# Where the first head's tiles lie: region order, a split weight load and an earlier product in a one-core decode kernel

## The chip, the cores and the metric

The kernel runs on one core of one Trainium2 chip. The metric is device time in microseconds (us). The core has a matrix engine (TensorE, "PE" in the profile, with its weight loads shown apart as "PEld"), VectorE ("DVE"), ScalarE ("ACT"), GpSimd ("POOL") and SyncE ("SP"), which here does nothing but issue loads. All engines run at once and wait for each other through semaphores. Loads from the chip's memory are carried by 16 DMA engines.

## The reference

One token of a decoder passes through an attention block and a gated MLP, and a scalar gate mixes the two:

```
g   = sigmoid((x * gate_w).sum())                       # x: 1 x 1024
q   = x @ wq                                            # 32 heads of 128
p   = softmax(q . k / sqrt(128))                        # 4 KV heads, 65536 cached rows
a   = (p @ v) @ wo
z   = gelu(x @ w_in)                                    # 1 x 3584, halves z1 and z2
u   = z1 * (w_sp * layernorm(z2) + b_sp)
b   = u @ w_out                                         # 1792 x 1024
out = g * a + (1 - g) * b
```

The caches `k_cache` and `v_cache` are bfloat16 of shape (1, 4, 65536, 128), 64 MiB each; 8 query heads share one of the 4 KV heads. The weights are 8 MiB (wq), 8 MiB (wo), 7 MiB (w_in) and 3.5 MiB (w_out). Every byte is read once, and there is one token to use it for.

## The kernel before

Almost everything that is loaded goes into one large buffer `kv` of 4 regions, 4 MiB each (32 KB in each of 128 partitions). The helper `load` issues a load on SyncE's queue into the place `at`, counted in regions; `load_kv` does it for one K tile (16,384 cache rows, one region) or a pair of V tiles (two regions). SyncE issues the loads in the order of the program. A load waits there until the earlier load into its region has landed and all its readers are done; loads behind it wait with it. The order of instructions on each engine is that of the program text (the last lines pin it).

The stages, in order:

- **w_in** in two halves to regions 2 and 3 (line 187), **wq** in one load to regions 0 and 1 (line 189). `x_rows` multiplies x with the first four of the eight row groups and then with the other four, so that two half views `wq_t` exist of the one load (line 190). From the products come `uT`, the vector for w_out, and `qs`, the queries, from which `build_w` makes the weights of the score matmuls.
- **Four KV heads**, g = 0 to 3, of NT = 4 K tiles each. `k_tile` (line 377) transposes a tile in four pieces on VectorE (line 383, the last reader of the region) and multiplies them on TensorE into `s_ps` (line 389); ScalarE copies the scores to SBUF (line 400).
- After a head's fourth tile, `stats` (line 403) finds the maximum over the scores. It needs TensorE twice: a transpose into `mt_ps` (line 408) and a matmul into `nb_ps` (line 415). Then come four exponentials on ScalarE (line 422) and four transposes on VectorE (line 425) that give `pt`.
- From the second head on, the V tiles of the head before are loaded in pairs into regions 2 and 3 and multiplied with `pt` in `v_tile` (line 435), beside the K tiles of the current head, which alternate between regions 0 and 1. `head_out` finishes a head.
- For the first head there are no V tiles yet, so its four K tiles use all four regions, in the order 2, 3, 0, 1 (line 488). After its statistics comes the load of **w_out** into region 2 and its product, 56 matmuls of `project` (line 477).
- **wo** in six loads, the last ones small, its product, and the output.

Of the kernel before, what the change touches and what calls it, by code (L numbers as in the profile page):

```python
# [17 lines left out]
NKV = 4  # L18
# [10 lines left out]
def kernel(  # L29
# [17 lines left out]
    _, _, D = A_x.shape  # L47
    _, G, S, DH = A_k_cache.shape
    HD = A_wq.shape[1]
# [4 lines left out]
    KC = D // P  # L54
    FC = FH // P
    OC = HD // P
    QD = P // H
    NT = S // (P * CT)
# [21 lines left out]
    def same_weights(ins):  # L80
        held.add(ins.ins.name)
# [77 lines left out]
    def load(src, shape, at):  # L159
        n = 1  # L160
        for s in shape:
            n *= s
        v = kv[:, int(at * CT * P):int(at * CT * P) + n]
        if len(shape) == 2:
            v = v.rearrange("p (a b) -> p a b", b=shape[1])
        ins = nc.sync.dma_start(out=v, in_=src)  # L166
        if not first_load:
            first_load.append(ins.ins.name)
        return v

    def load_kv(src, g, j, at, n=1):
        k0, m = j * CT * P, n * CT
        v = load(src[0, g, k0:k0 + m * P, :].rearrange("(p c) d -> p (c d)", c=m),
                 (m * DH,), at)
        return [v[:, i * CT * DH:(i + 1) * CT * DH] for i in range(n)]
# [9 lines left out]
    KH = KC // 2  # L185
    win_view = B_w_in.rearrange("(p c) n -> p c n", c=KC)
    win_t = [load(win_view[:, i * KH:(i + 1) * KH, :], (KH, F), 2 + i) for i in range(2)]
    wq_view = A_wq.rearrange("(p c) n -> p c n", c=KC)
    wq_a = load(wq_view, (KC, HD), 0)
    wq_t = [wq_a[:, i * KH:(i + 1) * KH, :] for i in range(2)]  # L190


    row = const.tile([P, P], FP32, name="row")
# [136 lines left out]
    uT = const.tile([P, FC], BF16, name="uT")  # L330
# [9 lines left out]
    for k in range(NHB):  # L340
# [3 lines left out]
                                                                   j=B, e=2),  # L344
# [20 lines left out]
    def build_w(g):  # L365
        for v in range(VC):
            nc.vector.tensor_tensor(
                out=wt[g % 2][:, v, :, :, v, :],
                in0=qs[:, g].unsqueeze(2).to_broadcast([P, BP, NB, REP]),
                in1=own_n[:].unsqueeze(1).unsqueeze(3).to_broadcast([P, BP, NB, REP]),  # L370
                op=ALU.mult)
# [5 lines left out]
    def k_tile(g, j, kn):  # L377
        kb = kn.bitcast(I32)
        n = CC * DH // 2
        s_ps = pss.tile([P, 2 * HN], FP32, name="s_ps", tag="s")  # L380
        for v in range(VC):
            kt = ktp.tile([P, CC * DH], BF16, name="kt")
            nc.vector.transpose(out=kt[:].bitcast(I32), in_=kb[:, v * n:(v + 1) * n])  # L383
            while late:
                nc.vector.reduce_max(**late.pop())  # L385
            kx = kt[:].rearrange("p (c h k e) -> p h e c k", h=2, k=B, e=2)
            for b in range(BP):
                for k in range(2):
                    ins = nc.tensor.matmul(  # L389
                        s_ps[:, k * HN:(k + 1) * HN],  # L390
                        lhsT=wt[g % 2][:, v, b].rearrange("p a v h -> p (a v h)"),
                        rhs=kx[:, b // 2, b % 2, k * CC // 2:(k + 1) * CC // 2, :],
                        start=(v == 0 and b == 0), stop=(v == VC - 1 and b == BP - 1),
                        skip_group_check=True)
                    if k > 0:
                        same_weights(ins)
        if j == 0:
            mxs[g] = wk.tile([P, NT], FP32, name="mx")
        sct[g, j] = scp.tile([P, CC * B], BF16, name="sc")
        nc.scalar.copy(out=sct[g, j][:], in_=s_ps[:])  # L400
        late.append(dict(out=mxs[g][:, j:j + 1], in_=sct[g, j][:], axis=AX.X))

    def stats(g):
        nc.vector.reduce_max(**late.pop())  # L404
        m1 = wk.tile([P, 1], FP32, name="m1")
        nc.vector.reduce_max(out=m1[:], in_=mxs[g][:], axis=AX.X)  # L406
        mt_ps = psm.tile([1, P], FP32, name="mt_ps", tag="m")
        nc.tensor.transpose(mt_ps[:], m1[:], ident_f[:])  # L408
        gm = wk.tile([1, REP], FP32, name="gm")
        nc.vector.tensor_reduce(out=gm[:], in_=mt_ps[:].rearrange("p (a h) -> p h a", h=REP),  # L410
                                axis=AX.X, op=ALU.max)
        gr = wk.tile([1, P // REP, REP], FP32, name="gr")
        nc.vector.tensor_copy(out=gr[:], in_=gm[:].unsqueeze(1).to_broadcast([1, P // REP, REP]))
        nb_ps = psm.tile([P, 1], FP32, name="nb_ps", tag="m")
        nc.tensor.matmul(nb_ps[:], lhsT=gr[:].rearrange("p a h -> p (a h)"),
                         rhs=ones_f[0:1, 0:1], start=True, stop=True)
        nb = wk.tile([P, 1], FP32, name="nb")
        nc.vector.tensor_scalar(out=nb[:], in0=nb_ps[:], scalar1=-SCALE, scalar2=None,  # L418
                                op0=ALU.mult)
        lss[g] = wk.tile([P, NT], FP32, name="ls")  # L420
        for j in range(NT):
            nc.scalar.activation(out=sct[g, j][:], in_=sct[g, j][:], func=ACT.Exp, scale=SCALE,  # L422
                                 bias=nb[:, 0:1], accum_out=lss[g][:, j:j + 1])
            ptt[g, j] = ptp.tile([P, CC, B], BF16, name="pt")
            nc.vector.transpose(out=ptt[g, j][:].rearrange("p c x -> p (c x)"),  # L425
                                in_=sct[g, j][:])

    def v_tile(g, j, vt):
        if j == 0:
            o_ps[g] = pso.tile([P, 2, VC * DH], FP32, name="o_ps")  # L430
        vx = vt.rearrange("p (v c d) -> p c v d", v=VC, d=DH)
        for u in range(CC // 2):
            hs = slice(u % 2 * P // 2, (u % 2 + 1) * P // 2)
            for e in range(2):
                ins = nc.tensor.matmul(  # L435
                    o_ps[g][hs, e, :],
                    lhsT=ptt[g, j][:, 2 * u:2 * u + 2, :].rearrange("p c x -> p (c x)"),
                    rhs=vx[:, 2 * u + e], start=(j == 0 and u < 2),
                    stop=(j == NT - 1 and u >= CC // 2 - 2), skip_group_check=True)
                if e > 0:  # L440
                    same_weights(ins)
# [32 lines left out]
    def project(w, n, vec, c0, first=False, last=False):  # L474
        for c in range(n):
            for t in range(NB):
                nc.tensor.matmul(  # L477
                    out_ps[t * B:(t + 1) * B, :],
                    lhsT=vec[:, c0 + c:c0 + c + 1].to_broadcast([P, B]),
                    rhs=w[:, c, t * NO:(t + 1) * NO],  # L480
                    start=(first and c == 0), stop=(last and c == n - 1),
                    skip_group_check=True)
# [2 lines left out]
    build_w(0)  # L485
    for g in range(G):
        for j in range(NT):
            k_tile(g, j, load_kv(A_k_cache, g, j, (j + 2) % NKV if g == 0 else j % 2)[0])
            if j == 1 and g + 1 < G:
                build_w(g + 1)  # L490
            if j == NT - 1:
                stats(g)
            if g > 0 and j % 2 == 1:
                for i, vt in enumerate(load_kv(A_v_cache, g - 1, j - 1, 2, 2)):
                    v_tile(g - 1, j - 1 + i, vt)
            elif g == 0 and j == NT - 1:
                project(load(B_w_out.rearrange("(p c) n -> p c n", c=FC), (FC, D), 2),
                        FC, uT, 0, first=True)
        if g > 0:
            head_out(g - 1)  # L500
    for j, n, at in ((0, 2, 0), (2, 1, 2), (3, 1, 3)):
# [58 lines left out]
```

## Time and profile before

| | |
|---|---|
| median of 5 runs | 384.12 us (383.99 to 384.16) |
| profiled execution | 384.12 us, its span 382.3 us |
| busy: PE, DVE, ACT | 233.1, 218.8, 39.6 us |
| DMA queue of SyncE | 162.01 MB, 98.7% of 16 engines' span |
| mean rate over the span | 424 GB/s |
| K tile loads | 16 of 4096 KB |
| K transposes on VectorE (line 383) | 64, mean 2280 ns |

The span is the time between the first and the last record of the profiled execution; 1.8 us of the execution lie outside it. A row of a timeline has the start and the length in us, the engine, the line of the kernel, the operation, what it writes and reads, how often it is repeated, and in brackets how long the engine had been idle before and what ended that. "SPq" is SyncE's queue issuing a load: its start is when the load was let go, not when its data moved. In the chain of waits, a line that begins with DMA runs from the issue of a load to its landing. The trace also holds a record of every DMA packet, with queue, size, start and length, and a 4-byte packet that each of the 16 DMA engines writes when its share of a load is done (here called a completion marker).

### The profile page before, as it was taken

The numbers are of one execution on the slowest core, as the hardware profiler recorded it, in microseconds if no ns is written. First come the engines' busy times: TensorE is split into PE (matmuls) and PEld (weight loads), VectorE is DVE, ScalarE is ACT, GpSimd is POOL, SyncE is SP. The second block draws the span as 40 slices with busy tenths as digits, with TensorE's granted clock in tenths as the row PEclk, the third lists the DMA queues.
The fourth block names the chain that finished last, engine by engine and source line by source line (L and its number), as shares of the span: only waits on it lengthen the run. The fifth ranks groups of instructions, "written<-read, shape, count | busy, mean of one in ns | idle before, by whom it ended". The sixth has DMA issues, their size and how long they took to land.

```text
span 382.3 us, 2628 instructions
## 1 busy us (share of the span) xinstructions
PE 233.1 (61%) x1372; PEld 60.2 (16%) x796; DVE 218.8 (57%) x211; ACT 39.6 (10%) x55; POOL 4.4 (1%) x10
## 2 busy tenths in 40 slices
PE   0430557675477957673977475648784975639354
PEld 0110111111211211120111011211120112112122
DVE  4241389996699178657890696559804976400040
ACT  1010001111601101140001011400110105000000
POOL 4000000000000000000000000000000000000000
PEclk9999969999578969968889899696897986959686
DMA  9998999999999999999999999999989999999995
GB/s 384 494 432 370 410 429 439 439 436 438 471 411 398 420 439 453 439 418 435 437 439 394 439 477 439 389 429 494 411 382 432 456 440 439 425 406 429 432 415 208
DMA packets 5095, 162.17 MB, mean 424 GB/s; under 512 B 600, under 2 KB 604, under 8 KB 988
## 3 DMA queue, kind: packets, MB, share of 16 engines
q1 hardware_dynamic: 5044, 162.01, 98.7%
q8 instruction: 8, 0.13, 0.1%
q14 instruction: 3, 0.02, 0.0%
q10 hardware_dynamic: 40, 0.01, 0.0%
HBM read 162.01 MB, written 0.00 MB: 424 GB/s over the span
## 4 chain that ended last, share of the span: by engine, by line
DMA 60%; DVE 17%; PE 16%; issue 4%; ACT 1%; SPq 0%; DVEq 0%; ACTq 0%
DMA kv<-in_A_v_cache_dram 31%; DMA kv<-in_A_k_cache_dram 16%; DVE kt L383 14%; PE o_ps L435 11%; DMA kv<-in_A_wo_dram 7%; DMA kv<-in_B_w_in_dram 5%; PE s_ps L389 4%; DVE pt L425 1%; PE z_ps L276 1%; ACT sc L400 1%; DVE o_sb L450 0%; SPq L166 0%; ACT L422 0%; ACT sc L422 0%; DVE om L446 0%
## 5 line engine op out<-in xcount | busy, mean ns | idle before, releaser
L389 PE MATMUL s_ps<-kt,wt 128*128 128x512 bf16 x512 | 137.1, 424 | 61.6 <-DVE kt L383 61.6
L383 DVE STREAM_TRANSPOSE kt<-kv 128x2048 int32<-128x2048 int32 x64 | 142.8, 2280 | 41.3 <-DMA kv<-in_A_k_cache_dram 41.2
L435 PE MATMUL o_ps<-kv,pt 128*64 128x512 bf16 x512 | 66.5, 425 | 22.1 <-DMA kv<-in_A_v_cache_dram 22.1
L389 PEld LDWEIGHTS <-wt 128*128 128x128 bf16 x256 | 26.9, 105 | 173.1 <-issue 132.5
L400 ACT CAST sc<-s_ps 128x1024 bf16<-128x1024 f32 x16 | 16.2, 1013 | 245.9 <-PE s_ps L389 245.9
L446 DVE TENSOR_TENSOR om<-o_ps,own 128x1024 f32<-128x1024 f32 x4 | 4.9, 1225 | 43.6 <-PE o_ps L435 43.6
L435 PEld LDWEIGHTS <-pt 128*64 128x64 bf16 x256 | 19.0, 122 | 67.4 <-issue 61.3
L425 DVE STREAM_TRANSPOSE pt<-sc 128x1024 bf16<-128x1024 bf16 x16 | 18.6, 1217 | 6.8 <-ACT sc L422 6.8
L422 ACT ACTIVATE sc<-sc,nb 128x1024 bf16<-128x1024 bf16 x16 | 18.2, 1136 | 10.1 <-DVE nb L418 10.1
L385 DVE TENSOR_REDUCE mx<-sc 128x1 f32<-128x1024 bf16 x12 | 14.5, 1209 | 7.7 <-ACT sc L400 7.6
L404 DVE TENSOR_REDUCE mx<-sc 128x1 f32<-128x1024 bf16 x4 | 4.9, 1220 | 12.8 <-ACT sc L400 12.8
L276 PE MATMUL q_ps<-kv,xT 128*32 128x512 bf16 x64 | 5.2, 498 | 10.8 <-DMA kv<-in_A_wq_dram 10.8
L477 PE MATMUL out_ps<-kv,oa 128*32 128x256 bf16 x128 | 7.0, 375 | 4.3 <-DMA kv<-in_A_wo_dram 2.8
L342 DVE TENSOR_TENSOR rowt<-q_ps,own_b 128x512 f32<-128x512 f32 x2 | 1.3, 684 | 13.9 <-PE q_ps L276 13.9
L456 PE MATMUL om_ps<-o_sb,hsel 128*32 128x128 f32 x8 | 1.6, 285 | 12.3 <-DVE o_sb L450 12.3
L276 PE MATMUL z_ps<-kv,xT 128*32 128x448 bf16 x64 | 6.4, 577 | 3.5 <-DMA kv<-in_B_w_in_dram 3.5
L450 DVE TENSOR_REDUCE o_sb<-om 128x128 f32<-128x1024 f32 x4 | 7.5, 1872 | 0.1
L408 PE MATMUL mt_ps<-ident_f,m 128*1 128x128 f32 x4 | 1.2, 296 | 10.2 <-DVE m L406 10.2
L516 ACT CAST out_sb<-out_ps 128x256 bf16<-128x256 f32 x1 | 0.4, 373 | 55.5 <-PE out_ps L477 55.5
L276 PEld LDWEIGHTS <-xT 128*32 128x32 bf16 x64 | 2.7, 131 | 21.4 <-issue 21.3
L290 DVE TENSOR_TENSOR rowt<-z_ps,own_b 128x448 f32<-128x448 f32 x2 | 1.2, 618 | 8.2 <-PE z_ps L276 8.2
L232 PE MATMUL xb_ps<-xg,spread 8*128 8x256 bf16 x1 | 0.4, 367 | 8.9 <-DMA xg<-in_gate_w_dram 8.9
(88 smaller groups left out, 61.8 us busy)
## 6 DMA issues: line engine op xcount, KB each, us to landing
kv<-in_A_k_cache_dram SPq DMA_DIRECT2D x16, 4096.0 KB, 26.2
kv<-in_A_v_cache_dram SPq DMA_DIRECT2D x2, 4096.0 KB
kv<-in_B_w_in_dram SPq DMA_DIRECT2D x2, 3584.0 KB, 14.8
kv<-in_A_wo_dram SPq DMA_DIRECT2D x1, 4096.0 KB, 22.7
kv<-in_B_w_out_dram SPq DMA_DIRECT2D x1, 3584.0 KB
kv<-in_A_wo_dram SPq DMA_DIRECT2D x1, 2048.0 KB
kv<-in_A_wo_dram SPq DMA_DIRECT2D x1, 1024.0 KB
kv<-in_A_wo_dram SPq DMA_DIRECT2D x1, 512.0 KB
```

The lines of the kernel that those rows point to most:

```text
L276: ins = nc.tensor.matmul(ps[t * B:(t + 1) * B, k * HN:k * HN + n], lhsT=xT[:, i * KH + c:i * KH + c + 1].to_broadcast([P, B]), rhs=w[:, c, ...
L383: nc.vector.transpose(out=kt[:].bitcast(I32), in_=kb[:, v * n:(v + 1) * n])
L385: nc.vector.reduce_max(**late.pop())
L389: ins = nc.tensor.matmul(s_ps[:, k * HN:(k + 1) * HN], lhsT=wt[g % 2][:, v, b].rearrange("p a v h -> p (a v h)"), rhs=kx[:, b // 2, b % 2, ...
L400: nc.scalar.copy(out=sct[g, j][:], in_=s_ps[:])
L404: nc.vector.reduce_max(**late.pop())
L422: nc.scalar.activation(out=sct[g, j][:], in_=sct[g, j][:], func=ACT.Exp, scale=SCALE, bias=nb[:, 0:1], accum_out=lss[g][:, j:j + 1])
L425: nc.vector.transpose(out=ptt[g, j][:].rearrange("p c x -> p (c x)"), in_=sct[g, j][:])
L435: ins = nc.tensor.matmul(o_ps[g][hs, e, :], lhsT=ptt[g, j][:, 2 * u:2 * u + 2, :].rearrange("p c x -> p (c x)"), rhs=vx[:, 2 * u + e], sta ...
L446: nc.vector.tensor_tensor(out=om8[:], in0=o_ps[g][:].rearrange("p e (v d) -> p (e v) d", d=DH), in1=own_8[:].unsqueeze(2).to_broadcast([P, ...
L450: nc.vector.tensor_reduce(out=o_sb[:], in_=om8[:].rearrange("p x d -> p d x"), axis=AX.X, op=ALU.add)
L477: nc.tensor.matmul(out_ps[t * B:(t + 1) * B, :], lhsT=vec[:, c0 + c:c0 + c + 1].to_broadcast([P, B]), rhs=w[:, c, t * NO:(t + 1) * NO], st ...
```

## The change

Four things change, and no byte that is loaded and no arithmetic.

- The first head's K tiles 0 to 3 go to regions 3, 0, 1, 2 instead of 2, 3, 0, 1.
- w_out goes to region 3 instead of region 2.
- wq is loaded in two halves, one to region 0 and one to region 1, instead of in one load over both.
- The product with w_out (with its load ahead of it) stands before the first head's `stats` instead of after it. On SyncE the order of the loads stays as it was; on TensorE the 56 matmuls now stand ahead of the statistics' transpose and matmul.

```diff
     wq_view = A_wq.rearrange("(p c) n -> p c n", c=KC)
-    wq_a = load(wq_view, (KC, HD), 0)
-    wq_t = [wq_a[:, i * KH:(i + 1) * KH, :] for i in range(2)]
+    wq_t = [load(wq_view[:, i * KH:(i + 1) * KH, :], (KH, HD), i) for i in range(2)]
...
         for j in range(NT):
-            k_tile(g, j, load_kv(A_k_cache, g, j, (j + 2) % NKV if g == 0 else j % 2)[0])
+            k_tile(g, j, load_kv(A_k_cache, g, j, (j - 1) % NKV if g == 0 else j % 2)[0])
             if j == 1 and g + 1 < G:
                 build_w(g + 1)
+            if g == 0 and j == NT - 1:
+                project(load(B_w_out.rearrange("(p c) n -> p c n", c=FC), (FC, D), 3),
+                        FC, uT, 0, first=True)
             if j == NT - 1:
                 stats(g)
             if g > 0 and j % 2 == 1:
                 for i, vt in enumerate(load_kv(A_v_cache, g - 1, j - 1, 2, 2)):
                     v_tile(g - 1, j - 1 + i, vt)
-            elif g == 0 and j == NT - 1:
-                project(load(B_w_out.rearrange("(p c) n -> p c n", c=FC), (FC, D), 2),
-                        FC, uT, 0, first=True)
```

## The prediction

> **What bounds the kernel now.** I read the head of the page first (busy shares, slices, DMA queues), to see which resource is full and whether it ever pauses.
>
> ```profile
> span 382.3 us, 2628 instructions
> PE 233.1 (61%) x1372; PEld 60.2 (16%) x796; DVE 218.8 (57%) x211; ACT 39.6 (10%) x55; POOL 4.4 (1%) x10
> DMA  9998999999999999999999999999989999999995
> q1 hardware_dynamic: 5044, 162.01, 98.7%
> q8 instruction: 8, 0.13, 0.1%
> q14 instruction: 3, 0.02, 0.0%
> ```
>
> No compute engine passes 61%. One DMA queue, SP's, holds packets on all 16 DMA engines for 98.7% of the span. The missing 1.3% is 5.0 us: the packet records put the first packet at 1.0 us and the last completion marker at 378.9 us, so 1.0 + 3.4 us of it are the two ends. Between them the records show no moment at which the queue ran empty.
>
> Second, the chain of waits in order of time. Its DMA pieces give start and length, so start plus length is a landing.
>
> ```profile
> 0.79 18.61 DMA kv<-in_B_w_in_dram
> ...
> 22.67 37.02 DMA kv<-in_A_k_cache_dram
> ...
> 134.67 30.59 DMA kv<-in_A_v_cache_dram
> ...
> 173.92 30.16 DMA kv<-in_A_v_cache_dram
> ...
> 211.26 31.97 DMA kv<-in_A_v_cache_dram
> ...
> 351.96 27.40 DMA kv<-in_A_wo_dram
> ```
>
> w_in lands at 19.40, K tile 1 of head 0 at 59.69, V pairs at 165.26, 204.08 and 243.23, the last load, of wo, at 379.37. From 59.69 to 165.26 six K tiles of 4 MiB, w_out (3.5 MiB) and two V pairs of 8 MiB land: 45.61 MB in 105.57 us, 432 GB/s. From 165.26 to 204.08 it is 16.78 MB in 38.82 us, again 432. So 4 MiB take 9.71 us, wherever they go and whatever the engines do meanwhile. All 162.01 MB at that rate are 375.0 us; the real stretch is 379.37 - 1.0 = 378.4 us. At most 3.4 us could be won by any order of loads.
>
> The packet records say where these 3.4 us are. The first packets (28 KB) took 1.60 to 2.01 us instead of 1.06, about 0.8 us. The rest is instruction fetches on queues 8 and 14: a 16 KB one takes 1.02 to 1.10 us of one DMA engine, and the 32 KB packet beside it takes 1.68 to 1.76 us instead of 1.22, so that engine is 1.5 us late from then on. A load lands when its latest engine is done. The spread of the 16 completion markers is 0.30 us up to wq, 1.81 from the fetch at 44.34 on, and 2.15 from 220 on, when an 8 KB fetch fell on an engine that had one already. None of it is a wait for a region.
>
> Third, the issues on SP's queue and the work around them (timelines of SP, PE and DVE):
>
> ```profile
> 16.00 6.99 SPq L166 DMA_DIRECT2D kv<-in_A_k_cache_dram  x2
> 42.34 0.33 SPq L166 DMA_DIRECT2D kv<-in_A_k_cache_dram  x1
> 44.07 0.33 SPq L166 DMA_DIRECT2D kv<-in_A_k_cache_dram  x1
> 58.98 0.33 SPq L166 DMA_DIRECT2D kv<-in_B_w_out_dram  x1
> 80.92 11.18 SPq L166 DMA_DIRECT2D kv<-in_A_k_cache_dram  x2
> 100.93 0.33 SPq L166 DMA_DIRECT2D kv<-in_A_v_cache_dram  x1
> 114.06 11.22 SPq L166 DMA_DIRECT2D kv<-in_A_k_cache_dram  x2
> ```
>
> ```profile
> 91.80 1.89 PE L389 MATMUL s_ps<-kt,wt 128*128 128x512 bf16 x8 [0.30 <-DVE kt L383]
> 96.24 0.27 PE L408 MATMUL mt_ps<-ident_f,m 128*1 128x128 f32 x1 [2.55 <-DVE m L406]
> 97.71 3.18 PE L477 MATMUL out_ps<-kv,uT 128*32 128x256 bf16 x56
> ```
>
> ```profile
> 136.31 2.31 DVE L383 STREAM_TRANSPOSE kt<-kv 128x2048 int32<-128x2048 int32 x1 [10.60 <-DMA kv<-in_A_k_cache_dram]
> ```
>
> By 9.71 us per 4 MiB from 59.69, head 0's K tiles 2 and 3 land at 69.4 and 79.1, w_out at 87.6, head 1's K tiles 0 and 1 at 97.3 and 107.0, the first V pair at 126.4, K tile 2 at 136.2 (DVE starts on it at 136.31, so the rule holds). Each load is issued while one or more are still queued. The margin (landing of the load ahead minus issue) is 6.1 us at the first V pair (107.0 - 100.9), 12.3 at the K tile issued at 114.06 (126.4 - 114.1), and over 5 at every other of these. A margin above zero costs nothing, and making it larger wins nothing.
>
> **The change part by part**, each against the time at which SP's queue would run dry.
>
> *Region order.* Head 0's K tile 0 goes to region 3, so it waits for the second half of w_in to be read: z_ps's second 32 matmuls start at 19.44 and take 3.18 us, so it is issued at 22.7 instead of 16.0. wq lands at 38.75 (the q_ps matmuls start at 38.80), so the margin falls from 22.7 to 16.0. Queued behind it on SP are tiles 1 to 3, which wait anyway. Cost 0; if w_in's product ended after 38, each us late would count.
>
> *wq in two loads.* The first half lands at 19.40 + 9.71 = 29.1. PE has nothing then but tot_ps (27.44); 32 q_ps matmuls follow, 3.5 us by the halves in before (38.80 to the issue at 42.34), so K tile 1 goes out at about 32.6 (22.7 before), ahead of the queue's running dry when tile 0 lands, at 50.0. After the second half PE does 32 matmuls instead of 64, so tiles 2 and 3 go out near 42.3 and 42.7 (42.34 and 44.07), and q and wt are ready about 2 us earlier. DVE gains nothing: tile 0 lands at 50.0 as before.
> The price of the split itself is 128 rows of 64 KB becoming 256 of 32 KB. Median packets: 64 KB 2.420 us, 32 KB 1.216 us; each of the 16 engines carries 8 rows, so 8 x (2 x 1.216 - 2.420) = 0.10 us, plus one completion marker of 0.01. No row shows two halves of wq, so I bound it: below, w_in's second load landed 8.33 us after its first against 8.49 at 432 GB/s, -0.16; above, the slow start of the first packets, +0.8. I take +0.1, by the packets of the same two sizes.
> The Trainium skill, "DMA: Bandwidth & Descriptors", section "Anatomy of one DMA", states a fixed cost of about 2.0 us per DMA besides bytes over 436 GB/s (fitted on the software path), which speaks against one more DMA; as an estimate from it the time would be 386.1. The K tiles of this trace stand 9.71 us apart with a load each, 4.19 MB at 432 GB/s, with no fixed part left over while the queue is full; by that row the sum stays at 384.2.
>
> *w_out in region 3.* It waits for K tile 0's transposes in both kernels and is issued at 59.0 in both. Cost 0.
>
> *Head 1's K tiles 0 and 1.* Regions 0 and 1 now hold head 0's tiles 1 and 2, whose transposes end one and two tiles earlier: issues at about 70.0 and 80.9 instead of 80.92 and 91.77. Margin rises by 11 us; gain 0, because the queue was full at 80.9 too.
>
> *w_out's product ahead of the statistics.* PE ends K tile 3 at 93.7, w_out has been there since 87.6, so the 56 matmuls (3.18 us) run from 93.7 to 96.9. The first V pair, which overwrites regions 2 and 3, goes out at about 97.0 instead of 100.9; margin 10 instead of 6 us, gain 0. The statistics' transpose on PE, ready at 96.24, waits for the product until 96.9: 0.7 us. Behind it wait nb, the four exponentials, the four pt transposes, then DVE's K transposes (105.19 to 105.9), so the next K issue is at 114.8 instead of 114.06: its margin is 11.6 instead of 12.3. DVE takes the 0.7 us back in its idle 10.60 us before 136.31. Cost 0; without that margin it would be 0.7 us.
>
> Sum: the profiled execution took 384.12 us, as did the median (span 382.3, 1.8 us around it). 384.12 + 0.1 = 384.2.
>
> **The rivals.**
> 1. Instruction fetches fall on other DMA engines, to the worse. In before the eight 16 KB fetches hit eight different engines. Were one to hit an engine that has one, the last engine would be about 3.3 us behind the first instead of 2.15 (2 x 1.5 + 0.3): +1.2, and 385.4. It decides from 0.77 us on. For it: the program is rebuilt, PE's early work moves. Against: number and order of instructions per engine stay the same but for one block, and eight different engines look like a rotation, not chance.
> 2. The same, to the better: the second 8 KB fetch misses the engine that already has one. The last engine is then 1.82 behind: -0.3, 383.9.
> 3. PE stands at w_out's product. If w_out landed after 93.7, PE, which works in order, would hold back statistics and everything behind them. It matters only beyond 6.1 us of lateness at PE and 11.6 us of margin at SP; a queue dry for 2 us would give 386.2. Nothing in the profile is that late.
> 4. Regions freed earlier shorten the end after all: most of the 3.4 us beyond the pure rate would have to be region waits, giving about 382. The packet records speak against it.
>
> **How the numbers follow.** Full queue with the fetches where they are, 0.77: 384.2 (own range 384.0 to 384.9, by the bounds of the split). Rival 2: 0.08; rival 1: 0.07; rival 3 or another dry queue: 0.05; rival 4: 0.03. About 0.2% (0.77 us) is what a measurement of this kernel tells from no change. Faster is rival 4, 0.03; slower is rivals 1 and 3, 0.12; same the rest, 0.85. The range runs from 383.7 (rival 2, less the lower bound of the split) to 385.0, leaving out rivals 1, 3 and 4: 0.15.
>
> **What would show it.** The share of queue q1 stays at 98 to 99% and the slices at 9 throughout; issues stand at about 22.7, 32.6, 42.3, 42.7, 59.0, 70, 81 and 97; the transpose of the statistics starts near 96.9 behind the 56 matmuls; head 0's second K tile still lands near 59.7 and the first V pairs' landings near 165.3 and 204.1; the last wo load near 379.4. The prediction is wrong if a slice of the DMA row falls below 8 between the ends, if landings drift from 9.71 us per 4 MiB, or if the spread of completion markers at the end is not near 2.2 us.

## The result and the profile after

| | before | after |
|---|---|---|
| median | 384.21 us (95 executions) | 384.00 us (52 executions) |
| mean | 384.78 us | 384.02 us |
| shortest and longest | 383.88 and 387.14 us | 383.80 and 384.51 us |
| executions above 384.6 us | 45 of 95 | 0 of 52 |
| profiled execution | 384.12 us, span 382.3 | 383.99 us, span 382.2 |

The ratio of after to before is 0.998, its 95% interval 0.9973 to 0.9987. That is the ratio of the two means. The two profiled executions differ by 0.13 us, the shortest of each kernel by 0.08. What the change removes is a tail: nearly half of the executions of before are 0.7 to 3.3 us longer than its shortest, and none of after is above 384.51. The five runs shown with the profile of before, 383.99 to 384.16, all came from the short half.

The head of the page of after, to be held against that of before:

```profile
span 382.2 us, 2629 instructions
PE 234.7 (61%) x1372; PEld 59.8 (16%) x796; DVE 218.7 (57%) x211; ACT 39.6 (10%) x55; POOL 4.4 (1%) x10
DMA  9999999999999999999999999899999999999995
q1 hardware_dynamic: 5188, 162.01, 98.7%
q8 instruction: 8, 0.13, 0.1%
q14 instruction: 3, 0.02, 0.0%
```

The share of SP's queue is what it was. The 144 packets more are wq's 128 rows cut in two and 16 completion markers. In the chain of waits, too, the landings stand where they stood:

```profile
22.87 27.30 DMA kv<-in_A_k_cache_dram
...
134.91 30.64 DMA kv<-in_A_v_cache_dram
...
352.12 27.21 DMA kv<-in_A_wo_dram
```

22.87 + 27.30 = 50.17 for head 0's first K tile, 165.55 for the second V pair, 379.33 for the last load of wo (379.37 before). SP's issues, in windows of its timeline so that each stands alone:

```profile
59.12 0.33 SPq L166 DMA_DIRECT2D kv<-in_B_w_out_dram  x1
70.32 0.33 SPq L166 DMA_DIRECT2D kv<-in_A_k_cache_dram  x1
81.17 0.33 SPq L166 DMA_DIRECT2D kv<-in_A_k_cache_dram  x1
95.63 0.33 SPq L166 DMA_DIRECT2D kv<-in_A_v_cache_dram  x1
114.11 0.33 SPq L166 DMA_DIRECT2D kv<-in_A_k_cache_dram  x1
```

Head 1's K tiles go out at 70.32 and 81.17 instead of 80.92 and 91.77, the first V pair at 95.63 instead of 100.93. In these two executions that moves nothing. The question for the experiments is what it does in the others.

### The profile page after: what moved, and what is told of

The parts are those of the page before. It is cut to its first block, busy times and chain, and to the rows that moved or that the text cites. A ratio compares the mean times of both kernels' runs of the same rounds, so it can differ in the third digit from the quotient of the medians.

```text
span 382.2 us, 2629 instructions
## 1 busy us (share of the span) xinstructions
PE 234.7 (61%) x1372; PEld 59.8 (16%) x796; DVE 218.7 (57%) x211; ACT 39.6 (10%) x55; POOL 4.4 (1%) x10
## 3 DMA queue, kind: packets, MB, share of 16 engines
q1 hardware_dynamic: 5188, 162.01, 98.7%
## 4 chain that ended last, share of the span: by engine, by line
DMA 57%; PE 21%; DVE 16%; issue 3%; ACT 2%; SPq 0%; DVEq 0%; ACTq 0%
DMA kv<-in_A_v_cache_dram 31%; DMA kv<-in_A_k_cache_dram 14%; DVE kt L382 13%; PE o_ps L434 11%; PE s_ps L388 8%; DMA kv<-in_A_wo_dram 7%; DMA kv<-in_B_w_in_dram 5%; DVE pt L424 1%; ACT sc L399 1%; PE z_ps L275 1%; DVE o_sb L449 0%; SPq L166 0%; ACT L421 0%; ACT sc L421 0%; DVE om L445 0%
## 5 line engine op out<-in xcount | busy, mean ns | idle before, releaser
L434 PE MATMUL o_ps<-kv,pt 128*64 128x512 bf16 x512 | 67.3, 429 | 20.6 <-DMA kv<-in_A_v_cache_dram 20.6
L275 PE MATMUL q_ps<-kv,xT 128*32 128x512 bf16 x64 | 6.8, 603 | 7.6 <-DMA kv<-in_A_wq_dram 7.6
```

The source lines that it names most:

```text
L275: ins = nc.tensor.matmul(ps[t * B:(t + 1) * B, k * HN:k * HN + n], lhsT=xT[:, i * KH + c:i * KH + c + 1].to_broadcast([P, B]), rhs=w[:, c, ...
L434: ins = nc.tensor.matmul(o_ps[g][hs, e, :], lhsT=ptt[g, j][:, 2 * u:2 * u + 2, :].rearrange("p c x -> p (c x)"), rhs=vx[:, 2 * u + e], sta ...
```

## The experiments

Two theories. **M (margin):** in the long executions of before, a load of head 1 is issued so late that the DMA queue has run dry, because TensorE's granted clock was low while head 0 was worked on. **F (fetches):** instruction fetches pile up on one DMA engine by chance, in any program.

### Each part alone

`e1_before` is the kernel before, unchanged. `e2_order` has the region order alone:

```diff
-            k_tile(g, j, load_kv(A_k_cache, g, j, (j + 2) % NKV if g == 0 else j % 2)[0])
+            k_tile(g, j, load_kv(A_k_cache, g, j, (j - 1) % NKV if g == 0 else j % 2)[0])
...
-                project(load(B_w_out.rearrange("(p c) n -> p c n", c=FC), (FC, D), 2),
+                project(load(B_w_out.rearrange("(p c) n -> p c n", c=FC), (FC, D), 3),
```

`e3_product` has w_out's product ahead of the statistics alone (w_out stays in region 2):

```diff
+            if g == 0 and j == NT - 1:
+                project(load(B_w_out.rearrange("(p c) n -> p c n", c=FC), (FC, D), 2),
+                        FC, uT, 0, first=True)
             if j == NT - 1:
                 stats(g)
...
-            elif g == 0 and j == NT - 1:
-                project(load(B_w_out.rearrange("(p c) n -> p c n", c=FC), (FC, D), 2),
-                        FC, uT, 0, first=True)
```

`e4_split` has wq in two loads alone:

```diff
-    wq_a = load(wq_view, (KC, HD), 0)
-    wq_t = [wq_a[:, i * KH:(i + 1) * KH, :] for i in range(2)]
+    wq_t = [load(wq_view[:, i * KH:(i + 1) * KH, :], (KH, HD), i) for i in range(2)]
```

> The kernel before, unchanged, to see its executions singly. What is to be explained: its 95 executions spread from 383.88 to 387.14 us with 47% above 384.6, those of the kernel after from 383.80 to 384.51 with none. Theory M (margin): in the long executions TensorE runs at a lower granted clock while head 0's tiles 2 and 3 and w_out's product are worked on, so that head 1's K tiles 0 and 1 (margins 6.7 and 5.6 us) or the first V pair (6.1 us) are issued after the DMA queue has run dry. It expects 30 to 60% of the executions above 384.6, up to 387. Rival F (fetches): instruction fetches pile up on one DMA engine in some executions of any program; then the spread is that of chance and every kernel of this call shows it, the parts alone too.

> Only the region order is changed (head 0's K tiles in 3, 0, 1, 2 and w_out in 3), wq in one load, w_out's product behind the statistics. Margins then: head 1's K tiles 17 and 16 us, first V pair 6.1 us as in before. Theory M: lateness of TensorE up to about 9 us still reaches the V pair, so a tail is left, of about the same length but in fewer executions (20 to 50% above 384.6). Theory F: as in before. If the tail goes away wholly, the K tiles' margins alone were at fault.

> Only w_out's product is put ahead of the first statistics (it stays in region 2, the K order stays 2, 3, 0, 1, wq in one load). Margins then: first V pair 10 us, head 1's K tiles 6.7 and 5.6 us as in before. Theory M: the K tiles' margins are still the smallest, the tail stays (30 to 60% above 384.6). Theory F: as in before. If the tail goes away, the V pair's wait for the product was the place.

> Only wq is loaded in two halves. Theory M: q is ready 2 us earlier, but head 0's K tile 0 lands at 50 us as before, so no margin from 60 us on changes and the tail stays (30 to 60% above 384.6); lowest executions within 0.2 us of before. If the tail goes away, it came from the start: wt ready later than 50 us in some executions, which pushes every later tile.

| kernel | median, us | shortest to longest | above 384.6 us |
|---|---|---|---|
| before, on the same chip | 384.41 | 383.88 to 386.75 | 17 of 35 |
| e1_before | 384.70 | 383.94 to 386.24 | 7 of 12 |
| e2_order | 384.09 | 383.88 to 385.84 | 4 of 12 |
| e3_product | 384.24 | 383.83 to 387.05 | 4 of 12 |
| e4_split | 384.68 | 383.92 to 385.55 | 6 of 12 |

No part alone removes the tail. Whether order and product alone make it rarer, 12 executions do not tell. The four ratios to before lie between 0.9996 and 1.0003, with intervals of about 0.2% to each side. The profile of e2 is of a short execution (383.93 us), so that its tail comes from the first V pair, which still goes out at 100.82, is argued and not shown.

The profile of e3 caught a long execution, 385.64 us, span 383.8. SP's issues of head 1's K tiles in it:

```profile
82.69 0.33 SPq L166 DMA_DIRECT2D kv<-in_A_k_cache_dram  x1
94.17 0.33 SPq L166 DMA_DIRECT2D kv<-in_A_k_cache_dram  x1
```

against those of before, in its profiled execution:

```profile
80.92 0.33 SPq L166 DMA_DIRECT2D kv<-in_A_k_cache_dram  x1
91.77 0.33 SPq L166 DMA_DIRECT2D kv<-in_A_k_cache_dram  x1
```

They are 1.8 and 2.4 us late. The windows of 5 us of e3 (window, its length, TensorE's busy time and matmuls, its granted clock, DMA share, GB/s) show both the cause and the effect:

```profile
55.00:60.00 5.00, 5.00 (x18) 0.74 1.05 452
...
65.00:70.00 5.00, 3.29 (x11) 0.78 1.02 439
70.00:75.00 5.00, 4.65 (x20) 0.87 1.00 433
75.00:80.00 5.00, 2.69 (x10) 0.81 0.92 394
80.00:85.00 5.00, 5.00 (x21) 0.85 1.04 447
...
95.00:100.00 5.00, 3.34 (x65) 1.00 0.98 370
```

and the same windows of before:

```profile
55.00:60.00 5.00, 5.00 (x23) 0.93 1.05 452
...
65.00:70.00 5.00, 3.79 (x16) 1.00 0.99 426
70.00:75.00 5.00, 3.80 (x16) 1.00 0.97 419
75.00:80.00 5.00, 3.15 (x15) 1.00 0.90 388
80.00:85.00 5.00, 4.40 (x19) 1.00 1.05 453
...
95.00:100.00 5.00, 3.05 (x47) 0.67 1.01 433
```

The granted clock is 0.74 instead of 0.93 from 55 to 60 us and 0.78 to 0.87 where before had 1.00, and after 95 us the DMA moves 370 instead of 433 GB/s. VectorE's timeline shows the way from the one to the other. The row maximum of a tile's scores stands on VectorE ahead of the last three transposes of the next tile, and it waits until TensorE has finished the scores and ScalarE has copied them. In e3 the maxima of head 0's tiles 0, 1 and 2 all wait for ScalarE:

```profile
63.22 1.22 DVE L385 TENSOR_REDUCE mx<-sc 128x1 f32<-128x1024 bf16 x1 [0.88 <-ACT sc L400]
74.83 1.22 DVE L385 TENSOR_REDUCE mx<-sc 128x1 f32<-128x1024 bf16 x1 [0.79 <-ACT sc L400]
86.31 1.22 DVE L385 TENSOR_REDUCE mx<-sc 128x1 f32<-128x1024 bf16 x1 [1.46 <-ACT sc L400]
```

In before only that of tile 2 does:

```profile
83.92 1.22 DVE L385 TENSOR_REDUCE mx<-sc 128x1 f32<-128x1024 bf16 x1 [0.83 <-ACT sc L400]
```

That is 3.13 us of waiting instead of 0.83, and the transposes that free the region end 2.4 us later. The packet records of e3 give the rest. The first DMA engine is done with the load ahead at 95.07, 0.90 us after the issue at 94.17; three engines that had to wait start on the late load at 96.01, 96.51 and 97.90, that is 1.8, 2.3 and 3.7 us after its issue. In before no packet record shows an engine without work at this place. The load's first completion marker comes at 105.55 instead of 104.84, its last at 108.58 instead of 106.66. The last load of wo then lands at 353.67 + 27.21 = 380.88 instead of 379.37. The DMA row of the page, in tenths of slices of 9.6 us, does not show it.

e4's profiled execution (385.08 us) shows a milder case: the same load is issued at 93.01, 2.2 us before the first engine is done (95.21), one engine starts on it only at 95.91 with a packet of 2.17 us, and a fetch of 16 KB at 103.78 then adds its 1.5 us to an engine that was late already. The spread of the markers goes from 1.80 to 2.71 us, later to 3.12. Whether that engine was late from the wait or from an earlier fetch the records do not say, since they do not name engines; theory F is not excluded by these runs alone. The profiled execution of e1 is the counterpart. Its load goes out as late, because VectorE waited 1.21 us for the scores at 63.43 (granted clock 0.69 from 55 to 60 us):

```profile
92.99 0.33 SPq L166 DMA_DIRECT2D kv<-in_A_k_cache_dram  x1
```

Yet it took 384.02 us. Three first packets were long (1.94 to 2.45 us), but the spread of the markers stayed at 1.80. An issue 2.2 us ahead of the first engine's end is thus on the edge, and what made e4's execution 1 us longer is open.

### Both parts, a fixed delay, and less work for TensorE

`e5_order_product` is e2 and e3 together, with w_out in region 3 and wq in one load. `e6_before_late` and `e7_after_late` add a delay on VectorE to before and to after:

```diff
+    spare = const.tile([P, 1], FP32, name="spare")
     build_w(0)
     for g in range(G):
         for j in range(NT):
+            if g == 0 and j == 2:
+                for _ in range(2):
+                    nc.vector.reduce_max(out=spare[:], in_=sct[0, 0][:], axis=AX.X)
```

`e8_before_half` is before with half of head 0's score matmuls:

```diff
-            for b in range(BP):
+            nb = BP // 2 if g == 0 else BP
+            for b in range(nb):
...
-                        start=(v == 0 and b == 0), stop=(v == VC - 1 and b == BP - 1),
+                        start=(v == 0 and b == 0), stop=(v == VC - 1 and b == nb - 1),
```

> Region order and w_out's product ahead of the statistics, wq in one load. Theory M, as sharpened by the packet records of the last runs: a load's first packets start 2.7 to 3.7 us after its issue, so that in before the loads of head 1's K tiles 0 and 1 and of the first V pair have only 4.5, 3.4 and 3.9 us from the issue to the moment at which the first DMA engine is done with the load ahead; a lower granted clock while head 0 is worked on eats the rest. With both parts these become 15, 14 and 9 us: no execution above 384.6, median 383.9 to 384.1. If the split counts, some executions stay above 384.6.

> Before, with two more row maxima (1.2 us each, result unused) on VectorE ahead of head 0's K tile 2: everything behind is 2.4 us later in every execution, whatever the clock does. Theory M: head 1's K tiles are issued at 83.3 and 94.2, 2.1 and 0.9 us before the first DMA engine runs dry; every execution is long, 385.3 to 387.5, none near 383.9. Theory F (fetches fall as chance has it): as before, shortest executions at 383.9 to 384.1.

> The kernel after with the same two row maxima. Theory M: head 1's K tiles at 72.7 and 83.6, the first V pair near 98, all over 6 us ahead: 383.9 to 384.2 as without them, none above 384.6. If the 2.4 us cost what they take: 386.4. Theory F: as after.

> Before, with half of head 0's score matmuls left out (two of the four blocks of weights; the scores of head 0 are not the reference's). TensorE then needs 3.4 us for a tile of head 0 at full clock and 6.8 at half, less than VectorE's 9 us for its transposes, so the clock no longer makes it late. Theory M: the tail of before goes away or nearly (at most 1 in 12 above 384.6), shortest executions about 383.9. Theory F, or a lateness that comes from elsewhere than TensorE: half of the executions stay above 384.6.

| kernel | median, us | shortest to longest | above 384.6 us | ratio to before |
|---|---|---|---|---|
| before, on the same chip | 384.69 | 383.90 to 386.77 | 17 of 32 | |
| e5_order_product | 383.90 | 383.77 to 384.09, and one of 482.12 | 0 of 11, and that one | 0.9977 (0.9961 to 0.9992) |
| e6_before_late | 385.74 | 384.49 to 388.17 | 10 of 12 | 1.0033 (1.0013 to 1.0053) |
| e7_after_late | 382.46 | 382.23 to 382.60 | 0 of 9 | 0.9945 (0.9927 to 0.9964) |
| e8_before_half | 384.04 | 383.95 to 384.12 | 0 of 12 | 0.9980 (0.9964 to 0.9996) |

One execution of e5 took 482.12 us; no profile of it exists, and its cause is open. The ratio leaves it out. Without it, e5 does all that the change does: **order and product together remove the tail, the split of wq is not needed.** The split's price, 0.1 us by the packets, has the sign of these medians (384.0 after, 383.9 here), but the same two kernels with 32 unused bytes (e9 and e11, below) differ by 0.06 us the other way: the runs do not resolve it.

e8 settles whose lateness it is. With half of TensorE's work in head 0 the tail is gone, while nothing in the order of loads, the regions or VectorE's work changed. From 65 to 80 us its granted clock is lower than e3's (columns as above), and still no row maximum of head 0's first three tiles waits; head 1's second K tile goes out before the moment at which the first engine is done (95.04), by over 4 us:

```profile
65.00:70.00 5.00, 3.73 (x8) 0.52 1.02 439
70.00:75.00 5.00, 2.73 (x8) 0.83 0.99 426
75.00:80.00 5.00, 3.33 (x8) 0.50 0.92 394
80.00:85.00 5.00, 2.38 (x9) 0.99 1.04 447
```

```profile
82.84 1.22 DVE L385 TENSOR_REDUCE mx<-sc 128x1 f32<-128x1024 bf16 x1
```

```profile
90.69 0.33 SPq L166 DMA_DIRECT2D kv<-in_A_k_cache_dram  x1
```

One thing else moves in e8: the instruction fetch at 101.46 in before stands at 110.01. That is not enough for theory F: in e3 this fetch is at 99.49, in after at 97.99, and e3 keeps its tail while after has none.

e6 and e7 brought a surprise: e7 is 1.5 us faster than after, which no theory had. Both have one more small tile than their bases, and it moved the load buffer `kv` in SBUF by 32 bytes. So e6 can only be read against a base with the same place; the next runs give it.

### The place of the load buffer

```diff
+    pad = const.tile([P, 8], FP32, name="pad")
     kv = big.tile([P, NKV * CT * P], BF16, name="kv")
```

The 32 unused bytes went into after (`e9_after_pad32`), before (`e10_before_pad32`) and e5 (`e11_order_product_pad32`); `e12_after_pad96` is after with `[P, 24]`, 96 bytes. No trace holds an address; the byte places below stand as the expectations give them.

> The kernel after with an unused 32-byte tile ahead of the load buffer, which moves the buffer (and what is allocated behind it) from byte 28128 of each partition to 28160, a multiple of 512. Theory P (place): the 1.5 us by which the late variant of after was shorter than after come from this place alone, since its result tile had moved the buffer there: 382.3 to 382.6, packets of 32 KB 1.213 us instead of 1.216, fetches 0.9 us instead of 1.07. Rival: they come from VectorE's delay; then 383.9 to 384.1 as after.

> Before with the same 32 bytes, for the comparison with the late variant of before, whose buffer stood there too. Theory M and P: shortest executions 382.3 to 382.6, and a tail of 1 to 3 us above them in a third to two thirds of the executions, as in before; the late variant, with 384.49 as its shortest, is then 2 us above its proper base in every execution. If alignment also removed the tail, the tail would be a matter of DMA pace and not of late issues.

> Region order, product ahead of the statistics, wq in one load, and the 32 bytes: the version meant to be shortest. Expected 382.3 to 382.5, 0.1 us under the after kernel with the 32 bytes (the split's price by the packets), no tail.

> After with a 96-byte tile: the buffer at 28224, a multiple of 64 but not of 128. If a multiple of 64 is enough: 382.3 to 382.6 like the 32-byte tile. If it needs more: 383.9 to 384.1, or between.

| kernel | `kv` at byte | median, us | shortest to longest | ratio to before |
|---|---|---|---|---|
| before, on the same chip | 28128 | 384.24 | 383.98 to 387.03 | |
| e9_after_pad32 | 28160 | 382.35 | 382.32 to 382.62 (5) | 0.9936 (0.9911 to 0.9961) |
| e10_before_pad32 | 28160 | 382.54 | 382.22 to 385.62 (12) | 0.9962 (0.9938 to 0.9987) |
| e11_order_product_pad32 | 28160 | 382.41 | 382.28 to 382.96 (6) | 0.9938 (0.9915 to 0.9961) |
| e12_after_pad96 | 28224 | 383.72 | 383.58 to 383.81 (12) | 0.9967 (0.9950 to 0.9983) |

The place alone is worth 1.65 us to after (384.00 to 382.35) and as much to the shortest executions of before (383.88 to 382.22). A multiple of 64 is worth 0.3 us. **e9 and e11 are shorter than both kernels and cannot be told from each other**; the 0.1 us that e11 was expected to be shorter did not appear. e11's longest execution, 382.96, is its profiled one: its first load lands 0.5 us later than in e9, and so does everything behind it, with no engine short of work. The queue of e9 is as full as that of after, and the span is shorter:

```profile
span 380.5 us, 2629 instructions
...
q1 hardware_dynamic: 5188, 162.01, 98.8%
```

Now e6 can be read: its shortest execution, 384.49, is 2.3 us above the shortest at the same place (e10, 382.22), and its issue is as late as M needs (94.2 expected):

```profile
94.87 0.33 SPq L166 DMA_DIRECT2D kv<-in_A_k_cache_dram  x1
```

2.4 us of lateness make all 12 executions of before long, while e7, with the same lateness, is 0.1 us from e9. The expected range of e6, 385.3 to 387.5, becomes 383.65 to 385.85 at this place, and the measured one, 384.49 to 388.17, reaches further up. e10 keeps its tail (5 of 12 above 382.95, which is 384.6 less 1.65), and its profile is again of a long execution, 385.62 us. e9's profile shows lateness too (VectorE is done with head 0's tile 2 at about 82.3, against 81.2 in after; in e10 at 82.6, against 80.9 in before), and it costs nothing, because the loads go out 11.9 us earlier. First e9, then e10:

```profile
70.67 11.94 SPq L167 DMA_DIRECT2D kv<-in_A_k_cache_dram  x2
```

```profile
82.57 11.88 SPq L167 DMA_DIRECT2D kv<-in_A_k_cache_dram  x2
```

(Two issues are merged in each line; the second ends it, so it starts at 82.28 and 94.12.)

## Why the prediction was wrong

The time, 384.2 us, was forecast within 0.2 us and lies in the range; the sign was not. I forecast no change with a tenth lost, and the change is a gain of 0.2% on the mean. That the time came out so near says little for the reasoning: the sum starts from a short execution of before, and after has only short ones. None of the signs that I had named for being wrong appeared in the profile of after (queue at 98.7%, landings as before, markers spread by 1.97 us), because all of them were read from short executions. Step by step:

- **The bound** was right: a full DMA queue, 4 MiB in 9.72 us, the ends as they were. Any kernel here that keeps the queue full at the old place has its shortest executions between 383.77 and 383.95.
- **The issues of after** were right within 0.7 us, but for the V pair, which went out 1.4 us earlier: 22.7, 32.6, 42.3, 42.7, 59.0, 70, 81, 97 and 114.8 forecast; 22.87, 32.70, 42.68, 43.15, 59.12, 70.32, 81.17, 95.63 and 114.11 measured. The 0.7 us wait of the statistics did not come, because the 56 matmuls took 1.71 us instead of 3.18 as the clock stood at 1.00 from 90 to 100 us (before, whose product ran later, had 0.67 from 95 and 0.50 from 100):

```profile
93.88 1.71 PE L476 MATMUL out_ps<-kv,uT 128*32 128x256 bf16 x56
96.49 0.27 PE L407 MATMUL mt_ps<-ident_f,m 128*1 128x128 f32 x1 [0.91 <-DVE m L405]
```

- **The split** was put at 0.1 us; the runs do not resolve it (e5 is 0.1 us below after, e11 0.06 above e9). Its other effect, q earlier by 1.4 us, reaches nothing, as said. The fixed cost of about 2.0 us per DMA that the Trainium skill, "DMA: Bandwidth & Descriptors", section "Anatomy of one DMA", states (a fit on the software path) is not added to a load in a full queue here: completion markers of successive K tiles of after stand 9.72 us apart, and those of the two halves of wq 9.70.
- **The margins were the step that failed**: "landing of the load ahead minus issue", over 5 us everywhere, so that "making it larger wins nothing". Two terms were left out. The queue runs dry when the *first* DMA engine is done, not when the load lands: for head 1's second K tile at 95.12, not 97.3, which leaves 95.12 - 91.77 = 3.35 us. And a load's first packets start 1.0 us after the issue on the first engines that wait for them (e6: issue 94.87, first packets from 95.84) and up to 3.7 us on another (e3). So the margin of 5.5 us (97.3 - 91.77) was really between 2.4 us and none.
- **One execution was taken for all.** The profile of before had the clock at 1.00 from 60 to 95 us, and the five times shown differed by 0.17 us. I saw the clock at 0.5 elsewhere in the same page and did not ask what it would do there. With a granted clock of 0.74 to 0.87 in e3, head 1's second K tile went out 2.4 us late, as much as the real margin at its best. e8 shows that it is TensorE's work, e6 that such a lateness is enough, e7 and e9 that after has room for it.
- **The rivals.** Rival 1 (fetches pile up) was not seen by itself: in every profiled execution whose queue did not run short the markers spread by 1.8 to 2.2 us at the end. In those that did run short it went up to 3.02 (e3), 3.12 (e4) and 3.63 (e10), but only to 2.30 in e6, which ended at 1.85. In e4 and e10 it grew again at later fetches; how much of a long execution is the shortage and how much this, was not taken apart. Rival 3 had the event, a queue that runs dry, but looked for it in after, where nothing is late; it happens in before. Rival 4 (earlier regions shorten the time) had the right sign but the wrong place: it looked for region waits within the 3.4 us of the short execution, where there are none, and not in the executions that were not shown.

## What to carry to other kernels

The slack of a prefetch is the time from its issue to the moment at which the first DMA engine runs out of work, less the time until its own first packets start on all engines (1.0 to 3.7 us here); what is left must cover the lateness that a lower clock can bring, not the lateness of the profile at hand. Where a full queue makes a change look worthless, the profile of a short execution cannot show its value: look at the spread of the times of many executions, and where a resource has a varying rate, ask what its worst rate does to the smallest margin. Then give the margin by reordering buffers, which here cost nothing that the runs could show.

## What the runs showed of the hardware that was not expected

- The place of the destination in SBUF counts for a full DMA queue. With `kv` at a multiple of 512 bytes (28160) instead of 32 bytes before it, a 32 KB packet takes 1.213 us instead of 1.216 (medians), a 64 KB packet 2.418 instead of 2.421, and a 16 KB instruction fetch beside them 0.88 to 0.97 us (e9) instead of 1.02 to 1.11 (after), though e3, at the old place, has one of 0.88 too; at 28224 it is 1.215 and 2.420. The 32 bytes move the tiles behind `kv` as well; that it is `kv`, which takes all the loads, is argued from the packets and not tried by itself. In after an engine carries 168 packets of 32 KB and 56 of 64 KB, so by the medians they make up 0.7 of the 1.65 us; the mean of all packet times of an engine on SP's queue falls by 1.25 us (377.33 in after, 376.08 in e9). The rest was not taken apart.
- The first packets of a load that is issued late are long, also where an engine shows hardly a gap. In e6 twelve of 1.70 to 1.99 us instead of 1.22 start between 95.84 and 96.16; in e3 ten of 1.53 to 1.93 start between 95.14 and 95.57, and one of 2.22 at 97.90, while the one at 96.51, after a wait, took 1.21. In before, with its issue 3.35 us ahead, none at this place is above 1.3. So late issues cost more than the gaps show.
